# Two feed-forward networks behind an attention on one core: seven block products in half of the second network's second layers, and all work placed by a list scheduler in the kernel

## The chip, the cores and the metric

One core of one Trainium2 chip. The metric is device time in microseconds of one execution, lower is better.

## What is computed

```python
qn = q / (np.linalg.norm(q, axis=1, keepdims=True) + 1e-06)
kn = k / (np.linalg.norm(k, axis=1, keepdims=True) + 1e-06)
s = kn.transpose(0, 2, 1) @ qn / tau
s = s - s.max(-1, keepdims=True)
a = np.exp(s)
a /= a.sum(-1, keepdims=True) + 1e-09
x = (v @ a).reshape(B * S, D)
...
h = x @ w_in
g = h * (1.0 / (1.0 + np.exp(-h)))
x = g @ w_out
...
h = x @ w_in
g = np.maximum(0.01 * h, h)
out = g @ w_out
```

There are 6016 tokens of 256 channels, and the hidden layers have 2048. All is float32. The attention matrix `a` is only 256 x 256, so it is folded into the first network's input weights, and nearly all of the work are the two networks of two layers each.

## The kernel before, in words

A float32 number is held as a high part (`gh`, `xh`, `wch`, `woh`) and a low part (`gl`, `xl`, `wcl`, `wol`), and a product of two blocks is three matmuls: high x high, high x low, low x high. The high part is a cast, which is ScalarE's (ACT's) work in most places, and the low part is the difference of the number and its high part, on VectorE (DVE).

The tokens are cut into six pairs of halves (`tpairs`): five pairs with 512 tokens a half, the last with 448. Each network passes over the pairs, and each pair takes eight steps, so there are 96 steps; a step covers 256 of the hidden channels. In a step, the first layer multiplies a 2 x 2 block of weights by a 2 x 2 block of tokens (halves by two blocks of channels) with seven products instead of eight, M1 to M7, in the order M5, M1, M6, M2, M7, M3, M4: 21 matmuls. Sums of weight blocks (`w_sum`) and of token blocks (`x_sum`) are made beforehand. The eight steps of the first pair use eight products ("plain").

Three of the eight PSUM banks, A, B and D (`trio`), take the products of a step. Between the products stand small instructions: `c5` copies M5 out of D, a copy of M1 starts bank B, the sum "da" (L504) writes A plus c5 into D after M6, the sum "d22" (L453) reads A plus c5 after M7 into an SBUF tile `hs`. M7 and M3 need da, M4 needs d22. Then the activation (`act`, L440 to L468) makes four parts of hidden values, "11", "22", "21" and "12", each with its cast and its low part (L462).

The second layer (`l2`, L526 to L543) of the step before is woven between the first layer's products: four parts by two blocks of output channels, eight products or 24 matmuls, into four banks `ps_y` that gather a pair's eight steps. After the last step of a pair `finish` (L545 to L561) empties the four banks: in the first network DVE copies them into tiles `o`, and SP's DMA queue stores them to `y_d`; in the second DVE transposes blocks of 32 x 32 and four stores of each go to the output.

The order is written by hand. A string `SLOTS` says for each step which slot is a product of the first layer and which of the second; all other work is put beside a slot with `put(k, slot, ...)`: the loads of `v` or `y_d` for the next pair (`load_v`, `load_y`, `turn_v`), its sums and splits (`x_sum`, `x_hi`, `x_lo`), and the reloading and splitting of the second network's weights (`reload_w`, `reload_wo`). From step 6 on the casts of tokens and weights are DVE's (`on_dve`). The tiles `hs`, `gh` and `gl` are rings of 3, 5 and 5; tiles of tokens and of outputs take homes from a shared list (`take`, `free`).

Of the kernel before, what the change touches and what calls it, by code (L numbers as in the profile page):

```python
# [19 lines left out]
def attention_moe_kernel(  # L20
# [63 lines left out]
    dpool = ctx.enter_context(tc.tile_pool(name="dpool", bufs=2))  # L84
# [5 lines left out]
    def f32(a):  # L90
        return a.bitcast(F32)
# [23 lines left out]
    on_dve = [False]  # L115

    def hi_of(hi, src):
        if on_dve[0]:
            nc.vector.tensor_copy(out=hi, in_=src)
        else:  # L120
            nc.scalar.copy(out=hi, in_=src)
# [6 lines left out]
    free = list(spots)  # L128

    def take(dtype, name):  # L130
        i = free.pop(0)
        return i, spots[i].tile([P, HT], dtype, tag=f"spot{i}", name=name)

    wch, wcl, woh, wol, wf = {}, {}, {}, {}, {}

# [30 lines left out]
    def x_hi(qi, i):  # L166
        n = tpairs[qi % NP][1]
        xh[qi][i], xl[qi][i] = take(F32R, "xh"), take(F32R, "xl")
        hi_of(xh[qi][i][1][:, :n], xf[qi][i][1][:, :n])
# [79 lines left out]
    n_first = len(jobs)  # L249
    for g in range(G):  # L250
        jobs += [w2i_piece(g, 0), w2i_piece(g, 1)]
# [61 lines left out]
    def job_lo():  # L313
        i = at["lo"]
        if i < at["hi"]:
# [66 lines left out]
    def w_hi(g, i, j, cs=slice(0, HG)):  # L382
        hi_of(wch[g][:, i:j, cs], wf[g][:, i:j, cs])
# [4 lines left out]
    def s4_hi(g):  # L388
        hi_of(wch[g][:, M3, :], s4[g][1])
# [16 lines left out]
    g_spots = {}  # L406
    owed = []

    g_n = [0]
    g_of, accs = {}, {}  # L410
# [5 lines left out]

    def widens(step):
        moe, p, s = step
        return s == 0 and tpairs[p][1] > tpairs[p - 1][1]

    def l1(step):
# [5 lines left out]
        cs = slice(fi * P, (fi + 1) * P)  # L427

        def group(ps, i, start, j=None):

            j = i if j is None else j
            ah, al = wch[g][:, i, cs], wcl[g][:, i, cs]
            bh, bl = xh[qi][j][1][:, :n], xl[qi][j][1][:, :n]
            for x, (a, b) in enumerate(((ah, bh), (ah, bl), (al, bh))):
                nc.tensor.matmul(  # L435
                    ps[:, :n], lhsT=a, rhs=b, start=(start and x == 0), stop=(x == 2),
                    skip_group_check=not start,
                )

        def act(part, ps, c=None):  # L440

            i = g_n[0] % 5
            h = mpool.tile([P, HT], F32, tag=f"hs{g_n[0] % 3}", name="hs")[:, :n]
            g_n[0] += 1
            if step in (steps[0], steps[-1]):
                got = take(F32R, "gh"), take(F32R, "gl")
                g_spots[part] = [i for i, _ in got]
                gh, gl = [t[:, :n] for _, t in got]
            else:
                gh = mpool.tile([P, HT], F32R, tag=f"gh{i}", name="gh")[:, :n]  # L450
                gl = mpool.tile([P, HT], F32R, tag=f"gl{i}", name="gl")[:, :n]
            if c is not None:
                nc.vector.tensor_tensor(out=h, in0=ps[:, :n], in1=c, op=ALU.add)  # L453
            src = ps[:, :n] if c is None else h
            if moe == 1:
                nc.scalar.activation(out=h, in_=src, func=AF.Silu)  # L456
            else:
                nc.scalar.activation(out=h, in_=src, func=AF.Prelu, alpha=0.01)  # L458
            g_of[step, part] = gh, gl

            def lo():
                nc.vector.tensor_tensor(out=gl, in0=h, in1=f32(gh), op=ALU.subtract)  # L462

            def split():
                nc.scalar.copy(out=gh, in_=h)  # L465
                return lo

            return split  # L468

        if plain(step):  # L470
            def halves(part):
                second, half = PARTS[part]
                ps = bank(next_h(), "ps_h")
                group(ps, M3 if second else M1, True, x_place(0, half))
                yield
                group(ps, M4 if second else M2, False, x_place(1, half))
                act(part, ps)()()
                yield

            todo = [halves(part) for part in (PARTS if s else ('11', '21', '22', '12'))]  # L480

            for t in todo + todo if s == 0 else [t for t in todo for _ in range(2)]:
                next(t)
                yield
            return

        a, d, b = trio
        trio[:] = b, d, a
        D = bank(d, "ps_d")
        group(D, M5, True)  # L490
        c5 = mpool.tile([P, HT], F32, tag="c5", name="c5")[:, :n]
        nc.scalar.copy(out=c5, in_=D[:, :n])  # L492
        yield
        A = bank(a, "ps_a")
        group(A, M1, True)
        B = bank(b, "ps_b")
        c1 = mpool.tile([P, HT], F32, tag="c1", name="c1")[:, :n] if widens(step) else None
        nc.scalar.copy(out=B[:, :n] if c1 is None else c1, in_=A[:, :n])
        for f in [f() for f in owed]:
            f()  # L500
        del owed[:]
        yield
        group(A, M6, False)
# [503 lines left out]
```

## Time and profile before

| | |
|---|---|
| runs, us | 1044.72, 1044.96, 1044.80; median 1044.8 |
| profiled execution, us | 1044.86 |
| its span, us | 1043.1 |
| mean granted clock of TensorE | 0.999 |
| TensorE (PE) busy | 1033.4 us in 4624 matmuls |
| DVE busy | 655.7 us in 1115 instructions |
| ACT busy | 609.3 us in 1100 instructions |
| bytes moved | 62.95 MB |

The span reaches from the first to the last instruction; the execution's own time is 1.76 us more. Busy time is the union of an engine's instructions, so it says how full an engine is, and the chain of waits says which of them sets the end.

### The profile page before, as it was taken

What the parts mean: (1) busy time and instruction counts of PE and PEld (TensorE: products, weight loads), DVE (VectorE), ACT (ScalarE), POOL (GpSimd) and SP (SyncE); (2) the same over time, 40 slices, a digit from 0 to 9 for tenths busy, and PEclk for the clock granted to TensorE, in tenths of its full rate; (3) what the DMA queues carried; (4) which work ended last, traced back from release to release, by engine and by line L of the source; (5) the groups of instructions that cost most, each with busy time, mean ns of one, the idle gap of its engine ahead of it and who ended that gap; (6) DMA issues with size and microseconds to landing.
All of it is one profiled execution on the core that took longest, in us unless ns stands there. A gap on an engine that the chain in (4) does not pass through costs nothing.

```text
span 1043.1 us, 12546 instructions
## 1 busy us (share of the span) xinstructions
PE 1033.4 (99%) x4624; PEld 865.3 (83%) x4624; DVE 655.7 (63%) x1115; ACT 609.3 (58%) x1100; POOL 13.6 (1%) x17
## 2 busy tenths in 40 slices
PE   9999999999999999999999999999999999999998
PEld 7778888888888888888998888888888888888997
DVE  5889787657656755755778755655654654653534
ACT  6789646565665566555555455555555455555553
POOL 2200000000000000000000000000000000000000
PEclk9999999999999999999999999999999999999999
DMA  9723523123114114002012113003002101200202
GB/s 353 282 80 105 118 51 91 33 71 99 31 51 122 30 31 117 11 21 91 21 55 90 33 31 71 1 11 68 4 11 52 20 10 32 35 1 1 41 1 36
DMA packets 115662, 62.95 MB, mean 60 GB/s; under 512 B 93328, under 2 KB 97680, under 8 KB 115600
## 3 DMA queue, kind: packets, MB, share of 16 engines
q1 hardware_dynamic: 111888, 61.69, 21.0%
q10 hardware_dynamic: 3712, 0.46, 0.3%
q8 instruction: 36, 0.59, 0.2%
q14 instruction: 26, 0.21, 0.1%
HBM read 45.61 MB, written 16.52 MB: 60 GB/s over the span
## 4 chain that ended last, share of the span: by engine, by line
PE 94%; DMA 3%; ACT 1%; DVE 1%; SPq 0%; issue 0%; ACTq 0%
PE ps_y L541 49%; PE ps_a L435 23%; PE ps_d L435 11%; PE ps_b L435 6%; PE ps_h L435 3%; DMA k_raw<-in_k_dram 2%; PE w_ps L348 1%; DMA q_raw<-in_q_dram 1%; DMA w_raw<-in_moe_w_in_dram 1%; SPq L599 0%; PE s_ps L612 0%; ACT gh L465 0%; ACT hs L456 0%; DVE gl L462 0%; DVE w_w L299 0%
## 5 line engine op out<-in xcount | busy, mean ns | idle before, releaser
L462 DVE TENSOR_TENSOR gl<-hs,gh 128x512 fp32r<-128x512 f32 (+1 forms) x384 | 252.8, 677 | 282.8 <-ACT gh L465 281.4
L541 PE MATMUL ps_y<-gh,wol 128*128 128x512 f32 (+1 forms) x768 | 295.9, 385 | 0.5 <-DVE wol L319 0.5
L541 PE MATMUL ps_y<-gl,woh 128*128 128x512 f32 (+1 forms) x768 | 295.9, 385 | 0.0
L541 PE MATMUL ps_y<-gh,woh 128*128 128x512 f32 (+1 forms) x768 | 295.8, 385 | 0.0
L465 ACT CAST gh<-hs 128x512 fp32r<-128x512 f32 (+1 forms) x384 | 225.5, 610 | 3.9
L541 PEld LDWEIGHTS ps_y<-gh,wol 128*128 128x128 f32 x768 | 144.2, 188 | 28.0 <-DVE wol L319 0.9
L541 PEld LDWEIGHTS ps_y<-gl,woh 128*128 128x128 f32 x768 | 144.2, 188 | 26.9
L541 PEld LDWEIGHTS ps_y<-gh,woh 128*128 128x128 f32 x768 | 144.2, 188 | 26.8
L435 PE MATMUL ps_a<-xh,wch 128*128 128x512 f32 (+1 forms) x352 | 136.2, 387 | 0.1
L435 PE MATMUL ps_a<-xl,wch 128*128 128x512 f32 (+1 forms) x352 | 135.5, 385 | 0.0
L435 PE MATMUL ps_a<-xh,wcl 128*128 128x512 f32 (+1 forms) x352 | 135.5, 385 | 0.0
L458 ACT ACTIVATE hs<-hs 128x512 f32<-128x512 f32 (+1 forms) x49 | 30.6, 624 | 109.3 <-DVE hs L453 109.3
L453 DVE TENSOR_TENSOR hs<-ps_a,c 128x512 f32<-128x512 f32 (+1 forms) x88 | 59.6, 678 | 42.5 <-PE ps_a L435 41.8
L492 ACT COPY c<-ps_d 128x512 f32<-128x512 f32 (+1 forms) x88 | 50.9, 579 | 50.5 <-PE ps_d L435 50.4
L435 PEld LDWEIGHTS ps_a<-xh,wch 128*128 128x128 f32 x352 | 66.1, 188 | 14.6 <-DVE hs L453 1.9
L435 PEld LDWEIGHTS ps_a<-xh,wcl 128*128 128x128 f32 x352 | 66.1, 188 | 12.4
L435 PEld LDWEIGHTS ps_a<-xl,wch 128*128 128x128 f32 x352 | 66.1, 188 | 12.0
L456 ACT ACTIVATE hs<-hs 128x512 f32<-128x512 f32 (+1 forms) x40 | 24.9, 622 | 78.8 <-DVE hs L453 78.8
L458 ACT ACTIVATE hs<-ps_b 128x512 f32<-128x512 f32 (+1 forms) x47 | 27.7, 590 | 71.6 <-PE ps_b L435 71.6
L504 DVE TENSOR_TENSOR ps_d<-ps_a,c 128x512 f32<-128x512 f32 (+1 forms) x88 | 60.5, 687 | 14.0 <-PE ps_a L435 12.7
L435 PE MATMUL ps_d<-xh,wch 128*128 128x512 f32 (+1 forms) x176 | 67.9, 386 | 0.0
L435 PE MATMUL ps_d<-xh,wcl 128*128 128x512 f32 (+1 forms) x176 | 67.8, 385 | 0.0
(113 smaller groups left out, 1174.5 us busy)
## 6 DMA issues: line engine op xcount, KB each, us to landing
w_raw<-in_moe_w_in_dram SPq DMA_DIRECT2D x16, 512.0 KB, 4.1
w_raw<-in_moe_w_out_dram SPq DMA_DIRECT2D x16, 512.0 KB, 3.7
y_d<-o SPq DMA_DIRECT2D x20, 256.0 KB, 2.0
xf<-y_d SPq DMA_DIRECT2D x20, 256.0 KB, 3.0
out_dram<-o SPq DMA_DIRECT2D x80, 64.0 KB, 1.9
q_raw<-in_q_dram SPq DMA_DIRECT2D x9, 512.0 KB, 9.9
k_raw<-in_k_dram SPq DMA_DIRECT2D x9, 512.0 KB, 9.9
v_raw<-in_v_dram SPq DMA_DIRECT2D x64, 64.0 KB, 2.4
```

The costliest lines, as they stand in the source:

```text
L348: nc.tensor.matmul(ps, lhsT=a[:, jc, m * P:(m + 1) * P], rhs=b[jc], start=(x == 0), stop=(x == len(order) - 1),)
L435: nc.tensor.matmul(ps[:, :n], lhsT=a, rhs=b, start=(start and x == 0), stop=(x == 2), skip_group_check=not start,)
L453: nc.vector.tensor_tensor(out=h, in0=ps[:, :n], in1=c, op=ALU.add)
L456: nc.scalar.activation(out=h, in_=src, func=AF.Silu)
L458: nc.scalar.activation(out=h, in_=src, func=AF.Prelu, alpha=0.01)
L462: nc.vector.tensor_tensor(out=gl, in0=h, in1=f32(gh), op=ALU.subtract)
L465: nc.scalar.copy(out=gh, in_=h)
L492: nc.scalar.copy(out=c5, in_=D[:, :n])
L504: nc.vector.tensor_tensor(out=D[:, :n], in0=A[:, :n], in1=c5, op=ALU.add)
L541: nc.tensor.matmul(ps, lhsT=a, rhs=b, start=(first and x == 0), stop=(last and x == 2))
```

## The change

In the second network, the second layers of steps with an even number are made with seven products. The four parts of hidden values give the forms T1 to T4 by differences on DVE (L561): T1 = "12" - "11", T2 = "22" - T1, T3 = "22" - "12", T4 = "21" - T2. Casts and lows are needed for seven forms where there were four: "11", "22", "21" and T1 to T4. Three sums of output weights (`wsh`, `wsl`) join the weights. Products P2, P3 and P4 go straight into banks `ps_y`. P1, P6, P7 and P5 go into the eighth bank, `ps_x`, which the first layers don't use, and DVE adds it to SBUF tiles E1, E2, E3 and E5 (L671; the first time in a pair ACT copies). P6 and P7 go on top of P1 in the bank, so E1, E2 and E3 read it between products. After the last even step of a pair (the seventh of the eight), six sums (`close`, L676) add the E's to the banks `ps_y`. The odd steps keep their eight products, and so does the first network.

From step 8 on (the second pair of the first network) nothing is put by hand any more. Each piece of work is a `Work` with an engine, a cost, the works that it depends on, homes that it needs, and a due time; a due time of DVE's and ACT's work is worked back from the product of PE that needs it. The scheduler keeps a clock for each engine, and takes again and again the work that could start first (among those almost equal, the one due first). Its outcome is the program's order on each engine. The first layer's products follow the old order; the second layer's are due a quarter of a step later than before. `hs`, `gh` and `gl` take homes from the shared list, which has 46 and later 49 of them. All casts made from step 8 on are ACT's.

```diff
@@ helpers @@
+    wsh, wsl = {}, {}
...
+    def seven(step):
+        return step[0] == 2 and step[2] % 2 == 0
...
+        def t1():
+            difference(hs[step, "11"], "12", "11")
+            hs[step, "T1"] = hs.pop((step, "11"))
...
+        def t2():
+            hs[step, "T2"] = home(step, "t2")
+            difference(hs[step, "T2"], "22", "T1")
...
+    DIRECT = {"P2": (0, 0, "21"), "P3": (0, 1, "22"), "P4": (1, 0, "T4")}
+    KEPT = {"P1": "11", "P6": "T2", "P7": "T3", "P5": "T1"}
+
+    def l2_seven(step, name):
+        moe, p, s = step
+        n = tpairs[p][1]
+        g = s // 2
+        at = {"P1": (0, 0), "P5": (0, 1), "P2": (2, 0), "P4": (2, 1)}
+        if name in at:
+            a = wo_at(g, *at[name])
+        else:
+            x = ("P6", "P7", "P3").index(name)
+            a = wsh[g][:, x, :], wsl[g][:, x, :]
+        if name in DIRECT:
+            m, half, form = DIRECT[name]
+            onto(step, m, half, a, form, False)
+        else:
+            form = KEPT[name]
+            if name in ("P1", "P5"):
+                kept["X"] = bank(H[3], "ps_x")
+            second_layer(step, kept["X"][:, :n], a, form, name in ("P1", "P5"), True)
+        used(step, form)
+
+    def keep(step, name, eng="dve"):
+        moe, p, s = step
+        n = tpairs[p][1]
+        x = kept["X"][:, :n]
+        if (p, name) not in kept:
+            kept[p, name] = take(F32, name)
+            hi_of(kept[p, name][1][:, :n], x, eng)
+        else:
+            e = kept[p, name][1][:, :n]
+            nc.vector.tensor_tensor(out=e, in0=x, in1=e, op=ALU.add)
...
+    CLOSE = ((0, 0, "E1"), (0, 1, "E2"), (1, 0, "E3"), (1, 1, "E3"), (0, 1, "E5"), (1, 1, "E5"))
...
+        SEVENS = ("P1", "P3", "P6", "P2", "P7", "P4", "P5")
...
+        LATE = {"pe": 0.2, "act": 0.13, "dve": 0.13, "sp": 3.0, "none": 0.0}
+        tt = lambda n: 0.061 + n * 0.001062
+        cp = lambda n: 0.061 + n * 0.000535
+        sc = lambda n: 0.098 + n * 0.00084
+        mm = lambda n: 3 * (0.2267 if n == HT else 0.2035)
...
+        BEHIND, PACE, AHEAD = 0.25, 1.0, 0.5
...
+            m6 = one("M6", [sd])
+            da = on("da", "dve", tt(n), [m6, c5])
...
+            m7 = one("M7", [da])
+            d22 = on("d22", "dve", tt(n), [m7, c5], homes=1, spare=4)
...
+        while left:
+            best = None
+            for e, q in queues.items():
+                q[:48] = [o for o in q[:48] if o.end is None]
+                mine = None
+                for o in q[:48]:
+                    if o.end is not None or o.release > reached or any(d.end is None for d in o.deps):
+                        continue
+                    if o.homes and len(free) < o.homes + o.spare:
+                        continue
+                    t = max([clock[e]] + [d.end for d in o.deps] + [home_at.get(i, 0) for i in free[:o.homes]])
+                    if o.bank is not None:
+                        t = max(t, bank_at.get(o.bank, 0))
+                    if mine is None or t < mine[0] - (0.02 if e == "pe" else 0.1):
+                        mine = t, o, e
+                if mine and (best is None or mine[0] < best[0]):
+                    best = mine
```

How the order moves is seen at three places. In the rows, a name before the arrow is what an instruction writes, those behind it what it reads.

First TensorE in an even step of the second network, from M6 (into `ps_a`) to M7 (into `ps_a` again). Before:

```order
3110 L435 MATMUL ps_a_6874<-xh_6213,wch_4974 128x512
3111 L435 MATMUL ps_a_6874<-xl_6214,wch_4974 128x512
3112 L435 MATMUL ps_a_6874<-xh_6213,wcl_4975 128x512
3113 L435 MATMUL ps_b_6878<-xh_6247,wch_4974 128x512
3114 L435 MATMUL ps_b_6878<-xl_6248,wch_4974 128x512
3115 L435 MATMUL ps_b_6878<-xh_6247,wcl_4975 128x512
3116 L541 MATMUL ps_y_6732<-gh_6833,woh_5124 128x512
3117 L541 MATMUL ps_y_6732<-gl_6834,woh_5124 128x512
3118 L541 MATMUL ps_y_6732<-gh_6833,wol_5125 128x512
3119 L541 MATMUL ps_y_6737<-gh_6833,woh_5124 128x512
3120 L541 MATMUL ps_y_6737<-gl_6834,woh_5124 128x512
3121 L541 MATMUL ps_y_6737<-gh_6833,wol_5125 128x512
```

Three more rows of `ps_y` follow before M7, which begins at row 3125. Now:

```order
3083 L438 MATMUL ps_a_7119<-xh_6452,wch_4941 128x512
3084 L438 MATMUL ps_a_7119<-xl_6453,wch_4941 128x512
3085 L438 MATMUL ps_a_7119<-xh_6452,wcl_4942 128x512
3086 L438 MATMUL ps_b_7135<-xh_6484,wch_4941 128x512
3087 L438 MATMUL ps_b_7135<-xl_6485,wch_4941 128x512
3088 L438 MATMUL ps_b_7135<-xh_6484,wcl_4942 128x512
3089 L617 MATMUL ps_x_7129<-gh_7109,wsh_5117 128x512
3090 L617 MATMUL ps_x_7129<-gl_7117,wsh_5117 128x512
3091 L617 MATMUL ps_x_7129<-gh_7109,wsl_5118 128x512
3092 L438 MATMUL ps_a_7119<-xh_6459,wch_4941 128x512
3093 L438 MATMUL ps_a_7119<-xl_6460,wch_4941 128x512
3094 L438 MATMUL ps_a_7119<-xh_6459,wcl_4942 128x512
```

M2 (`ps_b`) and P6 (`ps_x`) are left between M6 and M7, six matmuls where twelve stood.

Second DVE at the start of a pair of the first network, from the sum da (into `ps_d`) to d22 (into `hs`), with the transposes of the next pair's tokens (`xf` from `v_raw`). Before:

```order
321 L504 TENSOR_TENSOR ps_d_2350<-ps_a_2356,c5_2354 128x512
322 L190 STREAM_TRANSPOSE xf_2243<-v_raw_2258 128x512
323 L299 ISA w_w_2186<-w_w_2186,w_r_2187 128x1024
324 L190 STREAM_TRANSPOSE xf_2246<-v_raw_2263 128x512
325 L462 TENSOR_TENSOR gl_2391<-hs_2389,gh_2390 128x512
326 L453 TENSOR_TENSOR hs_2418<-ps_a_2356,c5_2354 128x512
```

Now:

```order
309 L690 COPY o_2368<-ps_y_1670 128x512
310 L303 ISA w_w_2174<-w_w_2174,w_r_2175 128x1024
311 L193 STREAM_TRANSPOSE xf_2225<-v_raw_2239 128x512
312 L193 STREAM_TRANSPOSE xf_2228<-v_raw_2244 128x512
313 L522 TENSOR_TENSOR ps_d_2349<-ps_a_2364,c5_2360 128x512
314 L193 STREAM_TRANSPOSE xf_2226<-v_raw_2331 128x512
315 L193 STREAM_TRANSPOSE xf_2227<-v_raw_2336 128x512
316 L542 TENSOR_TENSOR hs_2415<-ps_a_2364,c5_2360 128x512
```

Two transposes moved ahead of da, and all four stand ahead of d22; the low part that stood ahead of d22 follows it.

Third DVE at the very end of the program. Before:

```order
1092 L462 TENSOR_TENSOR gl_9277<-hs_9275,gh_9276 128x448
1093 L555 STREAM_TRANSPOSE o_9299<-ps_y_8762 128x448
1094 L555 STREAM_TRANSPOSE o_9311<-ps_y_8766 128x448
1095 L555 STREAM_TRANSPOSE o_9323<-ps_y_8782 128x448
1096 L555 STREAM_TRANSPOSE o_9335<-ps_y_8786 128x448
```

Now:

```order
1269 L671 TENSOR_TENSOR E5_9365<-ps_x_9890,E5_9365 128x448
1270 L694 STREAM_TRANSPOSE o_9902<-ps_y_9311 128x448
1271 L694 STREAM_TRANSPOSE o_9911<-ps_y_9337 128x448
1272 L676 TENSOR_TENSOR ps_y_9396<-ps_y_9396,E3_9335 128x448
1273 L676 TENSOR_TENSOR ps_y_9275<-ps_y_9275,E5_9365 128x448
1274 L694 STREAM_TRANSPOSE o_9928<-ps_y_9275 128x448
1275 L676 TENSOR_TENSOR ps_y_9396<-ps_y_9396,E5_9365 128x448
1276 L694 STREAM_TRANSPOSE o_9935<-ps_y_9396 128x448
```

Closing sums (L676) of the E's stand between the four transposes, one of them behind the last matmul and ahead of the last transpose.

## Rows read from the trace of the kernel before

**Rows 1.** Page, parts 1, 2 and 4: busy times, granted clock in tenths, chain's shares.

```profile
PE 1033.4 (99%) x4624; PEld 865.3 (83%) x4624; DVE 655.7 (63%) x1115; ACT 609.3 (58%) x1100; POOL 13.6 (1%) x17
...
PEclk9999999999999999999999999999999999999999
...
PE 94%; DMA 3%; ACT 1%; DVE 1%; SPq 0%; issue 0%; ACTq 0%
```

**Rows 2.** Chain in order of time, second network: start us, length us, engine, what, matmuls.

```profile
698.14 2.04 PE ps_y L541 x9
...
708.35 2.04 PE ps_y L541 x9
...
972.68 1.82 PE ps_y L541 x9
```

**Rows 3.** Waits of PE's weight loads and of DVE: us in total, times, longest us.

```profile
PEld ps_a L435 <- DVE hs L453: 1.9, 5, 0.4
...
DVE gl L462 <- ACT gh L465: 281.4, 211, 2.3
```

**Rows 4.** Window, one pair: PE, PEld, DVE, ACT, POOL busy us (x instructions); clock, DMA share.

```profile
647.00:728.00 81.00, 81.00 (x359) 67.11 (x358) 44.16 (x70) 44.50 (x80) 0.00 (x0) 1.00 0.12 26
```

**Rows 5.** Groups by shape from 647 us: busy us, mean ns of one, idle before.

```profile
L462 DVE TENSOR_TENSOR gl<-hs,gh 128x512 fp32r<-128x512 f32 x124 | 82.9, 690 | 111.9 <-ACT gh L465 111.2
L465 ACT CAST gh<-hs 128x512 fp32r<-128x512 f32 x124 | 73.6, 619 | 1.0
...
L504 DVE TENSOR_TENSOR ps_d<-ps_a,c 128x512 f32<-128x512 f32 x31 | 21.7, 700 | 4.8 <-PE ps_a L435 4.8
L453 DVE TENSOR_TENSOR hs<-ps_a,c 128x512 f32<-128x512 f32 x31 | 21.4, 691 | 20.9 <-PE ps_a L435 20.9
...
L492 ACT COPY c<-ps_d 128x512 f32<-128x512 f32 x30 | 17.7, 589 | 19.7 <-PE ps_d L435 19.7
```

**Rows 6.** Timeline of a step, DVE: start us, us to the last one's end, instruction.

```profile
703.29 1.29 DVE L462 TENSOR_TENSOR gl<-hs,gh 128x512 fp32r<-128x512 f32 x2 [1.69 <-ACT gh L465]
```

**Rows 7.** Timeline of the same step: the end of M6 and the sum da.

```profile
707.28 0.39 PE L435 MATMUL ps_a<-xh,wcl 128*128 128x512 f32 x1
...
707.70 0.70 DVE L504 TENSOR_TENSOR ps_d<-ps_a,c 128x512 f32<-128x512 f32 x1 [0.15 <-PE ps_a L435]
```

**Rows 8.** Timelines of SP and DVE at two pair starts; DMA issues, us to landing.

```profile
238.37 5.11 SPq L553 DMA_DIRECT2D y_d<-o  x4
243.53 4.22 SPq L185 DMA_DIRECT2D v_raw<-in_v_dram  x8
...
248.53 0.69 DVE L453 TENSOR_TENSOR hs<-ps_a,c 128x512 f32<-128x512 f32 x1 [0.32 <-PE ps_a L435]
...
639.77 8.63 SPq L561 DMA_DIRECT2D out_dram<-o  x16
...
out_dram<-o SPq DMA_DIRECT2D x80, 64.0 KB, 1.9
...
v_raw<-in_v_dram SPq DMA_DIRECT2D x64, 64.0 KB, 2.4
```

**Rows 9.** Timeline at a pair start of the first network: PE waits for d22.

```profile
178.09 0.68 DVE L453 TENSOR_TENSOR hs<-ps_a,c 128x512 f32<-128x512 f32 x1
...
178.44 0.39 PE L541 MATMUL ps_y<-gh,wol 128*128 128x512 f32 x1
...
179.16 0.39 PE L435 MATMUL ps_a<-xl,wch 128*128 128x512 f32 x1
```

**Rows 10.** Timeline of the end: lows on 448 tokens, last matmul, last transpose.

```profile
1031.13 1.16 DVE L462 TENSOR_TENSOR gl<-hs,gh 128x448 fp32r<-128x448 f32 x2 [1.53 <-ACT gh L465]
...
1032.64 0.63 DVE L462 TENSOR_TENSOR gl<-hs,gh 128x448 fp32r<-128x448 f32 x1 [0.35 <-ACT gh L465]
...
1037.69 0.37 PE L541 MATMUL ps_y<-gh,wol 128*128 128x448 f32 x1
...
1038.10 0.65 DVE L555 STREAM_TRANSPOSE o<-ps_y 128x448 f32<-128x448 f32 x1 [0.57 <-PE ps_y L541]
```

More of the change, by code (lines that the diff above doesn't have):

```diff
@@ L419, in widens, with product @@
         return s == 0 and tpairs[p][1] > tpairs[p - 1][1]
-    def l1(step):
+    def product(step, ps, i, start, j=None):
         moe, p, s = step
@@ L427, in l1 @@
         cs = slice(fi * P, (fi + 1) * P)
[L429 to L485, printed above, removed]
+        j = i if j is None else j
@@ new lines, in first_plain, with halves @@
+    def first_plain(step):
+        def halves(part):
+            second, half = PARTS[part]
+            ps = bank(next_h(), "ps_h")
+            product(step, ps, M3 if second else M1, True, x_place(0, half))
+            yield
+            product(step, ps, M4 if second else M2, False, x_place(1, half))
+            activated(step, part, ps[:, :tpairs[step[1]][1]])
+            yield
+        todo = [halves(part) for part in (PARTS if step[2] else ('11', '21', '22', '12'))]
+        for t in todo + todo if step[2] == 0 else [t for t in todo for _ in range(2)]:
+            next(t)
+            yield
@@ L487, in l1, with first_seven @@
+    def first_seven(step):
+        n = tpairs[step[1]][1]
         a, d, b = trio
         trio[:] = b, d, a
[L489 to L498, printed above, removed]
@@ new lines, in t4, with drop22 @@
+        def t4():
+            hs[step, "T4"] = home(step, "t4")
+            difference(hs[step, "T4"], "21", "T2")
+        def drop22():
+            free.append(hs.pop((step, "22"))[0])
+        ops = {
+            "M1": m1, "M2": m2, "M3": m3, "M4": m4, "M5": m5, "M6": m6, "M7": m7,
+            "c5": c5, "sd": sd, "da": da, "a11": a11, "d22": d22, "a22": a22,
+            "a12": lambda: straight("12", "D"), "a21": lambda: straight("21", "A"),
+        }
+        for part in PARTS:
+            ops["k" + part] = lambda part=part: cast(step, part)
+            ops["l" + part] = lambda part=part: lows(step, part, seven(step) and part in ("11", "22"))
@@ new lines, in second_layer, with used, wo_at @@
+    def second_layer(step, ps, a, form, first, last):
+        (hi, gh), (lo, gl) = g_of[step, form]
+        (ah, al) = a
+        for x, (a, b) in enumerate(((ah, gh), (ah, gl), (al, gh))):
+            nc.tensor.matmul(
+                ps, lhsT=a, rhs=b, start=(first and x == 0), stop=(last and x == 2),
+                skip_group_check=True,
+            )
+    def used(step, form):
+        free.extend(i for i, _ in g_of.pop((step, form)))
+    def wo_at(g, f, m):
+        ms = slice(m * P, (m + 1) * P)
+        return woh[g][:, f, ms], wol[g][:, f, ms]
@@ L540, in l2 @@
-        for x, (a, b) in enumerate(((ah, gh), (ah, gl), (al, gh))):
-            nc.tensor.matmul(ps, lhsT=a, rhs=b, start=(first and x == 0), stop=(last and x == 2))
-        if last:
-            finish(moe, p, m, half)
+        onto(step, m, half, wo_at(g, 2 * second + fi, m), part, last)
+        fed[step, part] = fed.get((step, part), 0) + 1
+        if fed[step, part] == KC:
+            used(step, part)
+    DIRECT = {"P2": (0, 0, "21"), "P3": (0, 1, "22"), "P4": (1, 0, "T4")}
+    KEPT = {"P1": "11", "P6": "T2", "P7": "T3", "P5": "T1"}
@@ L951, in attention_moe_kernel @@
[L951 to L962 removed]
+        wo_s = {}
```

506 lines of the change are left out of this document (397 added, 109 removed).

## The prediction

> **What bounds the kernel now.** I read the page's busy times and chain first. TensorE (PE) is busy 1033.4 of 1043.1 us, the granted clock is nine tenths or more of 2.4 GHz in every slice, and 94% of the chain that ended last are matmuls [rows 1]. So a microsecond is won only where matmuls go away or stop waiting. The chain in order of time gives the price of one: nine matmuls on 512 tokens take 2.04 us, 0.2267 us each, and nine on 448 take 1.82 us, 0.2022 each [rows 2]. The same nine come back 10.21 us later [rows 2], and 45 x 0.2267 is 10.20: a step is 45 matmuls (21 of its first layer, 24 of the second layer of the step before) with no gap. The waits say the same: what the weight loads of the first layer waited for on VectorE (DVE) is 1.9 us in 5 waits, while DVE itself waited 281.4 us for casts of ScalarE (ACT) [rows 3]. DVE is far from full: in an undisturbed pair of the second network it is busy 44.16 of 81 us, ACT 44.50 [rows 4]. That is the room that the change spends.
>
> **The matmuls that go.** In each even step of the second network the second layer has seven products of three matmuls, not eight. There are 6 pairs x 4 such steps; five pairs have 512 tokens a half and one 448. 20 x 3 x 0.2267 = 13.60 us and 4 x 3 x 0.2022 = 2.43 us, together 16.03 us less. No product is added elsewhere, and all of it lies on the path, since PE had no gaps to hide them in. First layers stay at 21 matmuls.
>
> **What DVE and ACT pay.** Durations come from the forms' means: a low part 0.69, a sum read from PSUM 0.69, one written to PSUM 0.70, a cast on ACT 0.62, a copy from PSUM 0.59 [rows 5]. Back to back, DVE starts the next low 0.60 after the one before (1.29 for two, less 0.69 for the last) [rows 6]. Per even step DVE gets 11 instructions more: three more lows, four differences (priced as lows, which also take two f32 operands from SBUF), four sums E from PSUM; ACT gets three casts more. Per pair six closing sums come on top, the four E's of the first step are ACT copies, and the seven casts of tokens go from DVE to ACT. So DVE goes from 70 to 70 - 7 + 44 - 4 + 6 = 109 instructions a pair, 109 x 0.60 = 65.4 us of a pair that shortens to 81.6 - 12 x 0.2267 = 78.9: 83%. ACT goes from 80 to 103, 44.5 + 23 x 0.62 = 58.8 us, 75%. Neither passes PE on the average of a pair, so I cost these instructions at nothing while PE's order covers them. If that cover went, the nearest price is one queued DVE instruction, 0.60.
>
> **Where the cover is thinnest.** PE waits for DVE inside a step at one close place: da, the sum that M7 and M3 need after M6. The last matmul of M6 began at 707.28 and DVE began at 707.70, 0.42 later, and da takes 0.70 [rows 7]. With 0.03 for the signal, M7 can begin 1.15 us after that matmul began. Before, twelve matmuls stood between M6 and M7; in the changed order six do (M2 and P6). Seven pitches are 1.59 us, so 0.44 us of slack is left, where there were 13 x 0.2267 - 1.15 = 1.80. One DVE instruction that begins just ahead of da can cost up to 0.60 - 0.44 = 0.16 us. Reading the order through several even steps by hand, with these durations, I find the queue empty at da in the steady ones. The bank ps_x is used by four products in turn (P1, P6, P7, P5), each time emptied by an E: 0.42 + 0.69 + 0.03 = 1.14 us from the product's last matmul, and nine matmuls usually stand between, 10 x 0.2267 = 2.27. That is covered as well.
>
> The Trainium skill's page "Perfetto Trace Analysis", section "Optimizing Tensor Performance", speaks against this part: "Independent matmul groups should rotate through different PSUM banks", so that one group is emptied under the next one's matmuls. By that rule, products straight behind each other in one bank would wait 1.14 - 0.23 = 0.91 us, 96 times, 87 us. The order puts other banks' products between them, by which the sum stays as it is.
>
> **The seams.** At the start of a pair in the first network, the order puts four transposes of v ahead of the sum d22 that M4 waits for, where two stood before; all four wait for transfers. Before, SP issued the four y stores from 238.37 (5.11 us) and then eight v loads (4.22 us); a v load lands 2.4 us after its issue, and d22 began at 248.53 [rows 8]. Now one y store (1.28) goes first and eight loads follow: 238.37 + 1.28 + 4.22 + 2.4 = 246.3, and two transposes later it is 247.5, a microsecond ahead of need. I take zero, with up to about 3 us each at four such seams if the loads get behind all four stores (5.11 - 1.28 = 3.8 us later, less the 1.0 in hand). In the second network the homes of the four output tiles are given to new tiles at once, which must wait for the output's stores: 16 stores are issued over 8.63 us from 639.77, and each lands after 1.9 [rows 8], so the last home is free some 11 us after the first transpose; the tiles that take them are wanted 8.6 to 11.2 us after it by the order. Some ACT work slips by half a microsecond, PE by none in my reading; the other end is 1 to 2 us at five seams. For seams and for the start of the second network, where the weights are converted (over two steps its count of DVE instructions there comes to more than 90% of the time), I put 0.5 us in all.
>
> **Old gaps.** The row of the weight loads' waits is 1.9 us in five places [rows 3]; at one of them the second matmul of M4 began at 179.16, two pitches after 178.44 would be 178.89, because d22 began as late as 178.09 and took 0.68 [rows 9]. The new order puts d22 by its due time, so these may go; I keep them, and let the range take them.
>
> **The tail.** Before, the last matmul began at 1037.69 and the last transpose ended at 1038.75, 1.06 later [rows 10]. Now each output bank needs its closing sums ahead of the transpose. After the last matmul one sum stands ahead of the last transpose (two lows on 448 tokens took 1.16, one 0.63, so 0.53 of DVE's time [rows 10]), the last products of bank (1, 1) wait until DVE has passed two transposes and a sum, some 0.5 us, and P5 waits some 0.2 us for E3: 1.2 us together. The sixteen stores and their landing behind it stay.
>
> **The sum.** 1043.1 - 16.03 + 0.5 + 1.2 = 1028.8 us of span. The profiled execution took 1044.86, 1.76 more than its span, and lies 0.06 above the median of the runs, 1044.8. 1028.8 + 1.76 = **1030.5 us**, 1.4% less. What a measurement of this kernel can tell from no change is about 0.2%, 2.1 us.
>
> **Rivals.**
> - *The scheduler also clears old gaps and the seams cost nothing.* For it: the order no longer puts sums of tokens ahead of d22. Then the 0.5 goes, the old 1.9 mostly too: about 1028.4. Chance 0.17.
> - *Seams wait for transfers.* For it: both kinds of seam have a microsecond or less in hand, and stores of several pairs share one SP queue. Against: four of the nine are as before but for the order of loads. At 0.8 to 1.5 us at most of nine seams it is 6 to 12 us: 1036 to 1042, nearer 1035 if only one kind waits. Chance 0.2.
> - *DVE comes late to da: the other side.* Place: M6 to M7 in each even step. Price: what is queued ahead of da, less 0.44. It turns the sign when the 24 steps lose the 14.3 us forecast and 2.1 more, 16.4 us or 0.68 each, which is two queued instructions (2 x 0.60 - 0.44 = 0.76): 24 x 0.76 = 18.2, about 1048.7. For it: DVE at 83%, and it takes its instructions in the order written, so that a low that waits for ACT holds da. Against: the due times put da first, and the order shows no two instructions ahead of it in a steady step. Chance 0.04.
> - *The products on ps_x wait for each other.* 0.91 us at each of the 96, 87 us: about 1118. Against: 2.27 us lie between them where 1.14 are needed. It decides from E's that begin 1.13 late, two queued DVE instructions. Chance 0.01. This is what the Trainium skill's rule on banks ("Perfetto Trace Analysis", "Optimizing Tensor Performance") would make of the time.
> - *The removed matmuls don't pay*, since something else sets the pitch: about 1046.5, with the tail and seams. Against: no other engine but the weight loads is over 63%, and 45 matmuls take 45 pitches. Chance 0.01.
>
> **How the numbers follow.** My forecast has 0.57, the rivals 0.17, 0.2, 0.04, 0.01 and 0.01. Its own spread is 1029.3 to 1033, from the tail without stalls (0.6) to a few missed da's. The range reaches down to 1028.2, where old gaps and tail stalls go, and up to 1036.5, which takes in the light half of the seams' case; above it lie 0.1 from the seams and 0.06 from the last three. Faster 0.95, same 0.02, slower 0.03.
>
> **What would show it.** The matmul count at 4552 and DVE near 109 instructions a pair. Even steps of 42 matmuls, 9.52 us at 512 tokens, in the chain; odd ones 10.20. Waits of the weight loads on da under 2 us in total. At the seams no wait of PE on a sum that stands behind transposes. The last transpose about 2.4 us after the last dense matmul. The forecast is wrong if even steps take over 9.7 us, or if PE's idle time past 150 us exceeds 4 us.

## The result, and the profile after

The changed kernel took 1030.44 us (median of 4 runs, 1029.88 to 1032.43) where 1030.5 was forecast; its ratio to the kernel before is 0.9866 (95% interval 0.9849 to 0.9883), 14.4 us less. Beside the last experiments it took 1030.56 against 1044.58, ratio 0.9864 (0.9849 to 0.9878). The time came out almost to the digit. The sum behind it did not: several of its terms were off, in both directions, so the digit is luck.

The page of the changed kernel, the lines that answer to [rows 1]:

```profile
PE 1017.8 (99%) x4552; PEld 851.2 (83%) x4552; DVE 776.4 (76%) x1313; ACT 716.7 (70%) x1298; POOL 13.6 (1%) x17
...
PEclk9999999999999999999999999999999999999999
...
PE 92%; DMA 4%; DVE 2%; ACT 1%; SPq 1%; issue 1%; ACTq 0%; DVEq 0%
```

72 matmuls are gone (4624 to 4552), PE is still busy 99% of the span and holds 92% of the chain. DVE rose from 655.7 to 776.4 us and ACT from 609.3 to 716.7, as the work added on them asks.

The chain in order of time, the product M2 of successive steps in the second network (start us, length us, what, matmuls), answers to [rows 2]:

```profile
651.87 0.69 PE ps_b L438 x3
...
662.09 0.68 PE ps_b L438 x3
...
671.61 0.68 PE ps_b L438 x3
...
741.10 0.68 PE ps_b L438 x3
```

From 651.87 to 662.09 it is a step with 45 matmuls, 10.22 us; from 662.09 to 671.61 one with 42, 9.52 us. The forecast had 10.20 and 9.52. From 662.09 to 741.10 it is a whole pair, 79.01 us, where 348 x 0.2267 is 78.89.

Windows of four successive steps (M2 to M2) and of a pair (columns as in [rows 4]):

```profile
730.90:741.10 10.20, 10.20 (x46) 8.45 (x46) 8.02 (x13) 7.18 (x13) 0.00 (x0) 1.00 0.01 2
741.10:750.62 9.52, 9.52 (x43) 7.89 (x43) 9.46 (x17) 7.45 (x14) 0.00 (x0) 1.00 0.00 0
750.62:760.84 10.22, 10.22 (x46) 8.35 (x46) 9.75 (x17) 8.93 (x17) 0.00 (x0) 1.00 0.00 1
760.84:770.36 9.52, 9.52 (x44) 7.84 (x43) 7.62 (x13) 5.70 (x10) 0.00 (x0) 1.00 0.01 2
...
711.00:790.00 79.00, 79.00 (x350) 65.15 (x349) 67.05 (x110) 57.03 (x103) 0.00 (x0) 1.00 0.12 27
```

The pair's row says that DVE is busy 67.05 of 79 us, 85%; the forecast was 83%. The four rows above it say what that average hides: DVE stands at 8.02 of 10.20, then at 9.46 of 9.52, then at 9.75 of 10.22, and at 7.62 of 9.52. In half of the steps DVE is full or nearly so (99% and 95%).

What PE's weight loads waited for past 150 us, the answer to [rows 3]:

```profile
PEld ps_a L438 <- DVE ps_d L522: 1.4, 7, 0.4
PEld ps_a L438 <- ACT ps_b L516: 0.9, 3, 0.4
PEld ps_a L438 <- DVE hs L542: 0.8, 3, 0.4
PEld ps_x L617 <- ACT E L120: 0.6, 1, 0.6
PEld ps_y L617 <- DVE ps_y L676: 0.4, 1, 0.4
PEld ps_x L617 <- DVE E L671: 0.2, 1, 0.2
```

Before, there were five waits for d22 (`hs`) of 1.9 us in all. They are 0.8 in three now, and in their place stand da (`ps_d`), copies by ACT, an E and a closing sum.

### The profile page after: what moved, and what is told of

It reads as the page before. It is cut to its first block, busy times and chain, and to the rows that moved or that the text cites. A ratio compares the mean times of both kernels' runs of the same rounds, so it can differ in the third digit from the quotient of the medians.

```text
span 1028.2 us, 12817 instructions
## 1 busy us (share of the span) xinstructions
PE 1017.8 (99%) x4552; PEld 851.2 (83%) x4552; DVE 776.4 (76%) x1313; ACT 716.7 (70%) x1298; POOL 13.6 (1%) x17
## 4 chain that ended last, share of the span: by engine, by line
PE 92%; DMA 4%; DVE 2%; ACT 1%; SPq 1%; issue 1%; ACTq 0%; DVEq 0%
PE ps_y L617 42%; PE ps_a L438 23%; PE ps_d L438 11%; PE ps_x L617 6%; PE ps_b L438 6%; PE ps_h L438 3%; DMA k_raw<-in_k_dram 2%; PE w_ps L353 1%; DMA q_raw<-in_q_dram 1%; DMA w_raw<-in_moe_w_in_dram 1%; SPq L738 0%; PE s_ps L751 0%; DVE gl L465 0%; DVE ps_y L676 0%; DMA out_dram<-o 0%
## 5 line engine op out<-in xcount | busy, mean ns | idle before, releaser
L465 DVE TENSOR_TENSOR gl<-hs,gh 128x512 fp32r<-128x512 f32 (+1 forms) x408 | 268.9, 676 | 64.5 <-ACT gh L120 62.8
L617 PE MATMUL ps_y<-gh,wol 128*128 128x512 f32 (+1 forms) x624 | 240.8, 386 | 0.5 <-DVE wol L324 0.5
L617 PE MATMUL ps_y<-gh,woh 128*128 128x512 f32 (+1 forms) x624 | 240.8, 386 | 0.0
L617 PE MATMUL ps_y<-gl,woh 128*128 128x512 f32 (+1 forms) x624 | 240.7, 386 | 0.0
L617 PEld LDWEIGHTS ps_y<-gh,wol 128*128 128x128 f32 x624 | 117.2, 188 | 22.8 <-DVE wol L324 1.0
L617 PEld LDWEIGHTS ps_y<-gh,woh 128*128 128x128 f32 x624 | 117.2, 188 | 22.3 <-DVE ps_y L676 0.4
L617 PEld LDWEIGHTS ps_y<-gl,woh 128*128 128x128 f32 x624 | 117.2, 188 | 21.9
L438 PEld LDWEIGHTS ps_a<-xh,wcl 128*128 128x128 f32 x352 | 66.1, 188 | 12.3
L451 ACT ACTIVATE hs<-ps_b 128x512 f32<-128x512 f32 (+1 forms) x47 | 27.7, 590 | 65.0 <-PE ps_b L438 64.9
L516 ACT COPY ps_b<-ps_a 128x512 f32<-128x512 f32 (+1 forms) x87 | 49.3, 567 | 31.4 <-PE ps_a L438 30.6
L438 PE MATMUL ps_d<-xl,wch 128*128 128x512 f32 (+1 forms) x176 | 67.8, 385 | 0.0
L449 ACT ACTIVATE hs<-ps_b 128x512 f32<-128x512 f32 (+1 forms) x40 | 23.5, 588 | 62.8 <-PE ps_b L438 62.8
```

Of the source, the lines that this page charges most:

```text
L438: nc.tensor.matmul(ps[:, :n], lhsT=a, rhs=b, start=(start and x == 0), stop=(x == 2), skip_group_check=not start,)
L465: nc.vector.tensor_tensor(out=lo[1], in0=h[1], in1=f32(got[0][1]), op=ALU.subtract)
L516: nc.scalar.copy(out=to, in_=got["A"][:, :n])
L617: nc.tensor.matmul(ps, lhsT=a, rhs=b, start=(first and x == 0), stop=(last and x == 2), skip_group_check=True,)
```

## The experiments

Each ran beside the kernel before on the same chip. All ratios are to that kernel. The changed kernel itself ran beside the last four only (1030.56 us); where an earlier run is compared with it in microseconds, the two may be from different chips, on which the kernel before took 1044.11 to 1044.58, so such a difference is good to about half a microsecond. PE's "stops" below are the time by which matmuls begin later than one pitch (0.2267 us, or 0.2027 on 448 tokens) after the one before, added up where that is over 14 ns.

**No step with seven products, the scheduler kept.** The products of the even steps then use a weight block that the sums have overwritten, so the second network's numbers are not the reference's; the work is what it would be.

```diff
-        return step[0] == 2 and step[2] % 2 == 0
+        return False
```

> Edit: no step of the second network uses seven products; the scheduler, the homes and the weight sums stay. If the gain is the 72 matmuls and nothing else, they come back at 16.0 us, while the tail's closing sums (1.1 us more after the last dense matmul than before) and the waits for E's (about 0.7 us in the changed kernel's trace) go: 1030.4 + 16.0 - 1.8 = 1044.6 us, within 0.2% of the kernel before. Rival, the scheduler's order has a gain of its own: old gaps of PE past 150 us (1.5 us) gone too, 1043.1; or, if half of the gain is the order's, about 1037.

Measured: 1042.83 us against 1044.28, ratio 0.9987 (0.9978 to 0.9997), so the new order, with the casts on ACT and the shared homes that come with it, is 0.3 to 2.3 us faster by itself. The waits of PE's weight loads past 150 us in its trace are one line:

```profile
PEld ps_a L438 <- DVE ps_d L522: 0.2, 1, 0.2
```

The five waits for d22 are gone. This is the rival that gave 1043.1. The products, then, are worth 1042.83/1044.28 to 1030.56/1044.58, 0.9986 to 0.9866: 12.6 us net. The 72 matmuls go at 16.0, and the seven products bring waits of their own: PE's stops past 150 us are 0.1 us in this trace and 2.2 in the changed kernel's.

**The sum da written two and three times.** It is the same value each time, so only DVE's queue is longer.

```diff
-            nc.vector.tensor_tensor(out=got["D"][:, :n], in0=got["A"][:, :n], in1=got["c5"], op=ALU.add)
+            for _ in range(2 if step[0] == 2 and step[2] % 2 else 1):
+                nc.vector.tensor_tensor(out=got["D"][:, :n], in0=got["A"][:, :n], in1=got["c5"], op=ALU.add)
```

> Edit: in the 24 odd steps of the second network (whose first layer is woven with a seven-product second layer) the sum da is written twice, with the same result; the order is otherwise the same. If da has 0.44 us in hand, one more DVE instruction at 0.60 costs 0.16 in each: 24 x 0.16 = 3.8 us, 1034.2. Rival, DVE is already what sets the pace there: the whole 0.60 is paid, 14.4 us, 1044.8. Rival, there is more in hand than I counted: 1030.4.

> Edit: as the run before, with da written three times. With 0.44 us in hand two more DVE instructions cost 2 x 0.60 - 0.44 = 0.76 in each of 24 steps, 18.2 us: 1048.6, slower than the kernel before, which is the price of the rival that the prediction gave for a slower kernel. If DVE already sets the pace: 28.8 us, 1059. If there is over 1.2 us in hand: 1030.4.

Measured: 1042.87 us, ratio 0.9989 (0.9980 to 0.9999), for one more; 1060.03 us, ratio 1.0152 (1.0137 to 1.0167), for two more. The first costs 1042.87 - 1030.56 = 12.3 us or 0.51 in each of 24 steps, the second 17.2 us or 0.71. The timeline of one such step, with one more:

```profile
705.44 0.39 PE L438 MATMUL ps_a<-xh,wcl 128*128 128x512 f32 x1
...
705.91 1.43 DVE L523 TENSOR_TENSOR ps_d<-ps_a,c 128x512 f32<-128x512 f32 x2
...
706.80 0.39 PE L618 MATMUL ps_x<-gh,wsl 128*128 128x512 f32 x1
...
707.39 0.50 PE L438 MATMUL ps_a<-xh,wch 128*128 128x512 f32 x1 [0.20 <-DVE ps_d L523]
...
707.73 0.39 PE L438 MATMUL ps_a<-xl,wch 128*128 128x512 f32 x1
```

The second da begins 0.73 after the first (1.43 less 0.70), not 0.60. PE's gap is 707.39 - 706.80 = 0.59 where the pitch is 0.23, and the next matmul comes 0.34 later instead of 0.23, so a stop costs 0.11 more at the restart. M7 begins 0.05 after da's end (705.91 + 1.43 = 707.34), where the prediction had 0.03 for the signal, so of 0.42 us between da and M7 only 0.37 can be used up: the bill here is 0.73 - 0.37 + 0.11 = 0.47. In the four such steps of this pair the trace shows 0.44, 0.47 twice and 0.69, on average 0.52, which is what was measured. The mechanism stands, and my price of 0.16 was a third of the real one.

**E's with homes of their own.**

```diff
-            kept[p, name] = take(F32, name)
+            if name not in e_home:
+                e_home[name] = take(F32, name)[0]
+            i = e_home[name]
+            kept[p, name] = i, spots[i].tile([P, HT], F32, tag=f"spot{i}", name=name)
...
-            free.append(kept.pop((p, name))[0])
+            del kept[p, name]
```

> Edit: the tiles E1, E2, E3 and E5 keep their four homes from pair to pair, so their first copies don't take the homes of output tiles that are still being stored. If the copies' wait for the output's stores makes the 0.5 us gap of PE at 806 us and the spread of the runs (1029.88 to 1032.43): PE has no gap over 0.2 us at the four seams, 1029.7 us, runs within 0.5 us of each other. Rival, other tiles take these homes and wait in their place (four homes fewer are free): 1030.4 or more, and the spread stays.

Measured: 1029.77 us (1028.62 to 1032.36), ratio 0.9867 (0.9849 to 0.9885): as the changed kernel. The waits for stores between 640 and 900 us, first in the changed kernel (us in total, times, longest):

```profile
ACT E L120 <- DMA out_dram<-o: 2.1, 3, 1.4
...
ACT gh L120 <- DMA out_dram<-o: 0.6, 1, 0.6
```

and with homes kept for the E's:

```profile
ACT gh L120 <- DMA out_dram<-o: 3.2, 4, 1.8
...
DVE gl L465 <- DMA out_dram<-o: 3.9, 2, 3.0
```

ACT's copies don't wait any more; its casts do, and DVE's lows with them. PE still had a gap at the same seam, 0.43 us between two matmuls at 805.56. The waits moved as the rival has it: whoever takes the output's homes waits. That the homes are too few is argued from this, as no run had more homes or faster stores; and the time can't choose between 1029.7 and 1030.4. The spread of the runs, 3.7 us, stayed too, but it says nothing about seams: the longest run has the lowest mean granted clock (0.996, the two shortest have 0.999). The profile of the changed kernel beside the last experiments shows where such time goes (1031.42 us, clock 0.997): the granted clock is 0.97 from 25 to 45 us and 0.93 from 45 to 60 us, and step 8 begins at 150.12, 1.1 us later than in the profile of 1029.99 us.

**Seven products in step 3 as well.**

```diff
-        return step[0] == 2 and step[2] % 2 == 0
+        return step[0] == 2 and (step[2] % 2 == 0 or step[2] == 3)
...
-            spots.update({i: more_pool[0] for i in range(HOMES, HOMES + 3)})
+            spots.update({i: more_pool[0] for i in range(HOMES, HOMES + 1)})
```

> Edit: step 3 of each pair of the second network uses seven products too (weight sums for it are added, and two of the homes go to make room). Three matmuls less in six steps: 5 x 0.68 + 0.61 = 4.0 us. DVE goes to 120 instructions a pair, 72 of 78 us. If DVE's queue still has da in time (0.15 to 0.46 us in hand in the changed kernel): 1026.4 us. Rival, DVE at 92% is late somewhere in most steps: 0.1 to 0.3 us in 40 steps, 1030 to 1038.

Measured: 1037.6 us, ratio 0.9936 (0.9919 to 0.9952), some 7 us slower than the changed kernel, with 18 matmuls less. A pair's window in its trace:

```profile
711.00:790.00 79.00, 78.74 (x343) 63.59 (x343) 72.81 (x120) 58.16 (x105) 0.00 (x0) 1.00 0.12 27
```

DVE is at 72.81 of 79 us and PE no longer at 79. A step with seven products gives DVE seven lows, four differences, four E's, da and d22: 17 x 0.60 = 10.2 us in a step of 9.52. It must borrow from the step after; steps 2, 3 and 4 in a row have nobody to borrow from. PE's stops past 150 us come to 12.8 us here, 5.0 of them from 590 to 652 us, in the first pair of the second network, and 1.4 to 1.6 in each pair after it. The two homes less may have their part in it; that was not tried alone.

**Token sums and lows on GpSimd, with four and with five such steps.**

```diff
-                s.append(Work("dve", tt(n), lambda eng, j=j: x_sum(qi, j), got + s))
+                s.append(Work(*(("pool", 1.4 * n / HT) if qi >= NP else ("dve", tt(n))), lambda eng, j=j: x_sum(qi, j), got + s))
...
-                X[qi, i] = Work("dve", tt(n), lambda eng, i=i: x_lo(qi, i), [h])
+                X[qi, i] = Work(*(("pool", 1.4 * n / HT) if qi >= NP else ("dve", tt(n))),
+                                lambda eng, i=i: x_lo(qi, i, nc.gpsimd if qi >= NP else None), [h])
```

> Edit: in the second network the four token sums and seven token lows of a pair go from DVE to GpSimd; seven products as in the changed kernel. DVE goes from 109 to 98 instructions a pair, 75% of the time. If PE's pitch is the bound and DVE costs only its lateness, at most the gaps of PE past step 8 go (2.3 us in the trace of the changed kernel): 1028.2 to 1030.4. If DVE's load by itself were the bound, 11 x 0.60 us in five pairs would come back: about 1000. Rival, GpSimd at work slows DVE's instructions: lows over 0.72 us on average, time over 1032.

> Edit: both of the two runs before: seven products in step 3 too, token sums and lows on GpSimd. DVE is back at 109 instructions a pair, 65 of 78 us. 4.0 us of matmuls less, and the gaps at most: 1025 to 1026.5 us. Rival, the two homes less or GpSimd's slower lows hold PE: 1030 or more.

Measured: 1038.85 us, ratio 0.9951 (0.9933 to 0.9968), and 1058.55 us, ratio 1.0139 (1.0116 to 1.0162). Taking 11 instructions of a pair off DVE made the kernel some 8 us slower. GpSimd's timeline and DVE's at two places of the first of the two:

```profile
594.43 7.84 POOL L123 TENSOR_TENSOR xl<-xf,xh 128x512 fp32r<-128x512 f32 x5 [37.90 <-ACT xh L120]
...
599.35 1.78 DVE L465 TENSOR_TENSOR gl<-hs,gh 128x512 fp32r<-128x512 f32 x1
...
601.06 1.77 DVE L561 TENSOR_TENSOR t<-hs 128x512 f32<-128x512 f32 x1
...
605.85 0.50 PE L438 MATMUL ps_a<-xh,wch 128*128 128x512 f32 x1 [2.09 <-ACT ps_b L516]
...
666.36 5.38 POOL L123 TENSOR_TENSOR xl<-xf,xh 128x512 fp32r<-128x512 f32 x3 [27.66 <-ACT xh L120]
...
667.00 0.69 DVE L522 TENSOR_TENSOR ps_d<-ps_a,c 128x512 f32<-128x512 f32 x1
667.60 1.18 DVE L465 TENSOR_TENSOR gl<-hs,gh 128x512 fp32r<-128x512 f32 x1
```

While GpSimd works from 666.36 to 671.74, one low takes 1.18 us instead of 0.68, straight behind da. While it works from 594.43 to 602.27, a low and a difference of DVE take 1.78 and 1.77; ACT's cast of that difference and its copy for bank B come late, and PE stands idle for 2.09 us. Past 545 us 37 instructions of DVE on 512 tokens that read SBUF alone overlap GpSimd's work by more than 0.3 us, and 17 of them take over 1.0 us; the 53 that read PSUM and overlap take 0.70 at most, and so do the 268 on SBUF that don't overlap. PE waits for GpSimd's own results nowhere in the second network. The Trainium skill's page "Perfetto Trace Analysis", section "Optimizing Scalar/DVE Operations", says that GpSimd and DVE share a read port of SBUF, so that moving work between the two might not help; these rows agree, and they give the price, 0.5 to 1.1 us on an instruction that it hits. So the rival holds. Its limit was met by a hair (from 560 us on the lows' mean rose from 686 to 722 ns), as a mean over many shows little of a few that are that late. In the second run 39 of 53 such instructions take over 1.0 us, and PE's stops past 150 us come to 33.0 us.

**The last pair without closing sums at its end.** Its last even step has eight products, with the overwritten block, so the last pair's numbers are not the reference's.

```diff
-        return step[0] == 2 and step[2] % 2 == 0
+        return step[0] == 2 and step[2] % 2 == 0 and step[1:] != (NP - 1, SS - 2)
```

> Edit: step 6 of the last pair uses eight products, so that its closing sums come two steps earlier. Three more matmuls on 448 tokens, 0.61 us; from the last matmul to the end of the span it takes 5.4 us as in the kernel before, not 5.84, and the three gaps of PE in the last 12 us (0.15, 0.08 and 0.32) go. Together 0.4 us less, about 1030.0, too little to see in one time; the trace tells. Rival: the closing sums hold PE two steps earlier instead, 1031.

Measured once: 1029.44 us. From the last matmul's start to the end of the span it takes 5.52 us, against 5.84 in the changed kernel and 5.39 before. The time fits the forecast, but the rows don't: the three gaps of the last 12 us are gone (0.55), and a stop of 0.24 us behind da at 1003.39 us is new, much as the rival had it. 0.61 - 0.32 - 0.55 + 0.24 come to nothing, so what this one time gains lies elsewhere.

**A low written twice, in the full steps and in the others.** The first repeats the low of T2 in even steps, the second the low of "12" in odd ones.

```diff
-        nc.vector.tensor_tensor(out=lo[1], in0=h[1], in1=f32(got[0][1]), op=ALU.subtract)
+        for _ in range(2 if seven(step) and form == "T2" else 1):
+            nc.vector.tensor_tensor(out=lo[1], in0=h[1], in1=f32(got[0][1]), op=ALU.subtract)
```

> Edit: the low part of form T2 of the even steps is written twice, 24 more DVE instructions. They run in the step after (the one in which the seven products are woven), ahead of da, where DVE's queue stood without idle time in the changed kernel's trace. If that stretch is what counts, and not the pair's average of 85%: da has 0.42 us in hand in one such step and 0.22 in the next, the instruction takes 0.60, and a stop of PE costs 0.11 more at its restart: 0.29 and 0.49, 24 x 0.39 = 9.4 us, 1039.8. If only the average counted: 1030.4.

> Edit: the low part of form 12 of the odd steps of the second network is written twice, 24 more DVE instructions too, but these run in the other half of the steps, where DVE stood idle for 2 us ahead of da. If the place counts: at most some 2 us, 1030.4 to 1032. If the load of DVE as such counted, it would cost as much as the run before, about 1040.

Measured: 1041.83 us, ratio 0.9977 (0.9967 to 0.9988), and 1038.65 us, ratio 0.9941 (0.9926 to 0.9955). The first costs 11.3 us, 0.47 a piece where 0.39 was expected. The second costs 8.1 us, 0.34 a piece, where I had expected at most 2 in all, so "the other half of the steps is idle" fell. Its timeline at a pair's end shows why:

```profile
712.14 1.41 DVE L466 TENSOR_TENSOR gl<-hs,gh 128x512 fp32r<-128x512 f32 x2
...
713.19 0.39 PE L438 MATMUL ps_a<-xh,wcl 128*128 128x512 f32 x1
...
713.46 1.29 DVE L677 TENSOR_TENSOR ps_y<-ps_y,E 128x512 f32<-128x512 f32 x2
...
714.66 0.69 DVE L523 TENSOR_TENSOR ps_d<-ps_a,c 128x512 f32<-128x512 f32 x1
...
715.40 0.50 PE L438 MATMUL ps_a<-xh,wch 128*128 128x512 f32 x1 [0.23 <-DVE ps_d L523]
```

The repeated low (1.41 for two) is followed by two closing sums, and da begins at 714.66, 1.47 after M6's last matmul began at 713.19; it should be 0.43. The work of the seven products spills over into the next step, and only where it has run out does DVE stand idle ahead of da. Of the first four such steps past 700 us in this trace three were late. The changed kernel's trace could have told: the idle 2 us stand ahead of da in one such step of four (at 691, 770 and 850 us), and in two of the four a closing sum or a token low runs right up to da, with 0.15 or 0.16 us left (at 711, 750, 790 and 830 us).

**The scheduler told of the stores.**

```diff
+            if getattr(o, "stores", False):
+                clock["sp"] = max(clock["sp"], o.end) + 4 * 0.54
             for i in free:
                 if i not in had:
                     home_at[i] = o.end
+            if getattr(o, "stores", False):
+                home_at[free[-1]] = clock["sp"] + 1.9
```

> Edit: the scheduler's clock is told that an output tile's home is free only when its four stores have been issued (0.54 us each on SP) and landed (1.9 us); ACT's order changes at the five pair starts of the second network (a copy E goes ahead of casts). If the waits of ACT for the output's stores (2.7 us in the middle of the second network) come from homes that the plan held free: they go, with PE's gaps of 0.5 and 0.25 at 806 to 810 us, and the time is 1029.6, under what two medians can tell. Rival, homes are too few and the waits move to other tiles: the waits stay near 2.7 us or more.

Measured: 1030.29 us, ratio 0.9860 (0.9846 to 0.9875), the same as the changed kernel beside it (0.9864). ACT's waits for stores in its trace:

```profile
ACT E L120 <- DMA out_dram<-o: 2.7, 4, 1.6
```

They are where they were: 2.7 us (2.1 and 0.6 in the changed kernel). A plan that knows of the stores does not free the homes any sooner.

> The changed kernel as it is, beside the others on the same chip: 1030.4 us, and the same gaps of PE past the start of the second network, for every comparison of these runs.

Measured: 1030.56 us. No version that I ran is faster than the changed kernel by more than the runs can tell.

## Why the prediction was right, point by point

**The matmuls that go: right.** Steps of 42 matmuls take 9.52 us and 72 matmuls are gone from a PE that stays at 99%.

**The slack at da: right in size, wrong in how much of it is free.** Two steps of the changed kernel (answering to [rows 7]), M6's last matmul, da, and M7's first:

```profile
661.70 0.39 PE L438 MATMUL ps_a<-xh,wcl 128*128 128x512 f32 x1
...
662.17 0.69 DVE L522 TENSOR_TENSOR ps_d<-ps_a,c 128x512 f32<-128x512 f32 x1
...
663.28 0.39 PE L438 MATMUL ps_a<-xh,wch 128*128 128x512 f32 x1
...
681.45 0.39 PE L438 MATMUL ps_a<-xh,wcl 128*128 128x512 f32 x1
...
681.53 0.69 DVE L465 TENSOR_TENSOR gl<-hs,gh 128x512 fp32r<-128x512 f32 x1
...
682.13 0.70 DVE L522 TENSOR_TENSOR ps_d<-ps_a,c 128x512 f32<-128x512 f32 x1
...
683.04 0.40 PE L438 MATMUL ps_a<-xh,wch 128*128 128x512 f32 x1
```

In the first, da ends at 662.86 and M7 begins at 663.28: 0.42 us in hand, as worked out (0.44). In the second a low stands straight ahead of da (681.53), da begins 0.68 after M6's last matmul and 0.21 us is left, from which 0.05 for the signal goes. The step of the prediction that failed is "I find the queue empty at da in the steady ones". From 690 to 870 us the hand left to M7 runs from 0.15 to 0.46 us, and PE loses next to nothing. The order was planned with about these durations (0.605 us for an instruction of DVE), which is the likely reason; no run shows it alone. What was free in my count is the scheduler's to fill.

**The shared bank: covered.** The waits of PE's weight loads on `ps_x` are 0.6 us for ACT's first copies and 0.2 for DVE's sums E, in the whole second network. The prediction's rival had 87 us, for products straight behind each other; with other banks' products between them this trace shows 0.8. The Trainium skill ("Perfetto Trace Analysis", "Optimizing Tensor Performance") wants independent groups of matmuls to rotate through the PSUM banks; this trace agrees.

**The price of the rival: too low.** The prediction had the sign turn at two DVE instructions ahead of da in each of 24 steps. One repeated da took the gain to 0.9989, nearly all of it, and two gave 1.0152, slower. The mechanism and the place were right; the price lacked the restart (0.11), the signal (0.05 for 0.03), the longer repeat (0.73) and, in some steps, the hand already spent.

**The old gaps: wrong.** I kept 1.9 us of waits that the new order removes: the run without seven products shows them gone, and is faster than the kernel before by 0.3 to 2.3 us. This was a rival of chance 0.17, and it held in part.

**The seams: mechanism right, size a third of the real one.** I had 0.5 us, with the start of the second network. The seam near 806 us is the place where the homes are short (SP's stores, then ACT and PE):

```profile
795.07 9.52 SPq L700 DMA_DIRECT2D out_dram<-o  x16
...
806.11 0.59 ACT L120 COPY E<-ps_x 128x512 f32<-128x512 f32 x1 [1.42 <-DMA out_dram<-o]
806.14 0.39 PE L438 MATMUL ps_d<-xh,wcl 128*128 128x512 f32 x1
...
806.75 0.50 PE L617 MATMUL ps_x<-gh,woh 128*128 128x512 f32 x1 [0.23 <-ACT E L120]
```

ACT's copy of an E waits 1.42 us for a store, out of 16 that took 9.52 us to issue where they took 8.63 before [rows 8]. The next product on `ps_x` begins 0.61 after the matmul before it, 0.38 late. PE's weight load waits 0.6 us there; in the run beside the experiments it was 1.0. After two of the four seams (at 651 and 810 us) ACT's copies come late once more and PE loses 0.2 each time; the other two seams cost it nothing. Beside this stand waits where the second network's weights are converted, so that gaps of over 14 ns beyond the pitch, from step 8 to the last 12 us, come to 1.7 us, of which the seams are 0.9 and the weights 0.6; before, such gaps were 1.6. The loads of the first network's seams cost nothing, as forecast.

**The tail: right.** The end of the changed kernel answers to [rows 10]:

```profile
1020.60 1.28 DVE L676 TENSOR_TENSOR ps_y<-ps_y,E 128x448 f32<-128x448 f32 x2
...
1020.84 0.37 PE L617 MATMUL ps_y<-gh,wol 128*128 128x448 f32 x1
...
1021.25 0.47 PE L617 MATMUL ps_y<-gh,woh 128*128 128x448 f32 x1
...
1022.37 0.37 PE L617 MATMUL ps_y<-gh,wol 128*128 128x448 f32 x1
1022.77 0.63 DVE L676 TENSOR_TENSOR ps_y<-ps_y,E 128x448 f32<-128x448 f32 x1 [0.22 <-PE ps_y L617]
1023.44 0.65 DVE L694 STREAM_TRANSPOSE o<-ps_y 128x448 f32<-128x448 f32 x1
```

The last transpose ends at 1024.09, 1.72 after the last matmul's start, where it was 1.06, by the closing sum at 1022.77. PE stops at 1021.25 for 0.21 behind a closing sum, and the smaller stops of the last 12 us bring that to 0.55. As the span's end came 0.45 later after the last matmul (5.84 for 5.39), the tail costs 1.0 us; I had 1.2. Two numbers beside that sum were off: the sign "about 2.4 us after the last dense matmul" is 1.72 after the last one, as the stops lie ahead of it, and the low end of the forecast's own spread, 1029.3, does not follow from a tail of 0.6, which gives 1029.9.

**The sum as it was.** From 1043.1: -16.0 for the matmuls, -1.6 for the old gaps, +1.7 for new ones, +1.0 for the tail, +0.4 for delays below 14 ns on matmuls of 512 tokens (in the second network 108 of them come 3 to 14 ns late), -0.1 for the matmuls on 448 tokens, -0.3 because step 8 began earlier in this execution: 1028.2, which is the span. I had -16.0, 0, +0.5 and +1.2: 1028.8. Old gaps that went and new ones that came cancel by luck, which the number alone would never have told. The -0.1 hides something larger. In both traces the matmuls on 448 tokens begin 202.7 ns apart in some stretches and 206.7 in others, at a granted clock of 1.00 in both: before in the last pair of the first network (some 0.7 us from 507 us on), now in that of the second (some 0.6 us, from 975 to 1006 us). What sets it is open; no experiment bears on it.

## What to carry to other kernels

Where an engine off the critical path is filled up to pay for work taken off the bound one, look at its load step by step, not by the average: here 85% over a pair was 99% over a step, and one more instruction in every two steps cost PE 0.34 to 0.51 us, in whichever of the two it was put. Slack that is counted by hand in the old order belongs to whoever places the work in the new one. And when a forecast is right, run the halves of the change apart before believing its terms.

## What was not expected of the hardware

A matmul that follows a stop takes 0.34 us to the next one instead of 0.23, so each stop costs 0.11 us beyond its length. An instruction of DVE that repeats the one before, into the same tile, begins 0.73 us after it, where independent ones are 0.60 apart. GpSimd at work made lows and differences of DVE take up to 1.78 us instead of 0.68, about half of those that overlap it, and none of the instructions that read PSUM.
